# Windowed attention with a rational feed-forward layer: the score matmuls of two half blocks interleaved over the four quarters of the TensorE array

## The chip, the cores and the metric

The kernel runs on one core of a Trainium2 chip. The metric is the device time of one execution in microseconds (us), smaller being better. The kernel before took 675.06 us (median of 3 runs, 675.04 to 675.08). One further execution was taken with the hardware profiler on; every row of a profile in this document comes from such an execution.

## The reference

Inputs are q, k and v of 4 batches, 8 heads, 768 positions and head dimension 64, and the weights of a feed-forward layer. What is computed, in short:

```python
block, window, scale = 32, 16, 1 / sqrt(64)
k_sum = k in blocks of 32, max over the block          # 24 per head
v_sum = v in blocks of 32, mean over the block
scores_l = scale * q @ k.T, masked to |i - j| < 16
scores_s = scale * q @ k_sum.T + log(32)
a = softmax(concat(scores_l, scores_s))
x = (a @ concat(v, v_sum)) as (3072 tokens, 512)
h = x @ w_in                                            # 2048 wide
g = (a0 + a1 h + a2 h^2 + a3 h^3) / (1 + |b0| |h| + |b1| h^2)
out = g @ w_out
```

## The kernel before

**Two halves of work.** The feed-forward layer takes 6 groups of 512 tokens; each group runs over 16 slices of the hidden width, so there are 96 steps (the loop at line 523), and a step's second layer is issued three steps later (`LAG`). Its numbers are split into a high and a low part, so each step has 12 matmuls of 128x128 by 512 for `h` (`moe1`, line 364) and 12 for `po` (`moe2`, line 403). Between them lies the gelu-like function of a step (`gelu`, line 376): on ScalarE (ACT) tiles `tq`, `ta`, `tu` from `h`, on VectorE (DVE) products of `tu` with `h`, and `gh`; on GpSimd (POOL) `gl`. `h` has two buffers in PSUM (`ps_h`), so the matmuls of `h` two steps on wait until DVE has read `h` for the last time, in `tu<-tu,cs,h`.

**The attention** is made in half blocks of 64 queries, 48 of them, numbered `jj`; eight give the tokens of one group. A half block sees 96 keys around its queries and 24 block maxima, 120 columns (`NK`). Its 8 heads lie in 4 head pairs (`NPAIR`): of a pair, head e = 0 lies on SBUF partitions 0 to 63 and head e = 1 on 64 to 127, for q (`qw`) and for the keys (`kw`). `scores` (line 195) is a generator. First it issues 8 matmuls, for each pair `pr` and each `e`, with q as the stationary operand (64x64) and the keys as the moving one (64 rows, 120 columns), in full fp32, into partitions `e * 64` to `e * 64 + 63` of one PSUM tile `sc` (one bank, 480 of 512 columns used). Such an fp32 matmul is two records in the trace, since TensorE makes it in two passes; in the compiled program the two passes of a matmul stand one behind the other. Then DVE adds the mask and takes each row's minimum (4 reads `ss<-sc,mask`, one for each pair), ACT makes the exponentials (4, `ss<-ss,sm`), DVE the reciprocal of the sum, and POOL multiplies by it.

**What follows a half block.** `turned` transposes `ss` on TensorE with an identity (`pt`), ACT copies it out as `pts`, 120 keys on partitions and, for each pair, 64 queries of e = 0 and then 64 of e = 1 along the columns. `both_values` (line 284) multiplies with the values of two half blocks at once: 16 fp32 matmuls `av`, each of 120 rows, 64 columns of the array and 64 moving columns, where e selects the output partitions and the columns of `pts`.

**Order.** Up to step 13 all engines follow an order written out by hand (`EARLY`, `STEP`); half blocks 0 to 15 are done there, and there `scores` issues its own matmuls, before and after the change. From step 14 (`NSTRICT`) only TensorE (PE) keeps the order of the text, and a scheduler orders ACT, DVE and POOL. In this part, every fourth step (14, 18, ..., 74, sixteen of them, `start_of` at line 506) makes the scores of two half blocks, 16 to 47 in pairs. PE's order in such a step is: 12 matmuls of `h`, 16 of `av` for the two half blocks of four steps before (from step 18 on), the 16 of `sc`, 12 of `po`. The transposes of the first of the two half blocks stand two steps later between the `po`, those of the second three steps later. PSUM tiles `sc` and `pt` share a pool of two buffers (`ps_a`).

Lines of a helper that records every operation (`Kept`) stand as L85 in all rows, so instructions are told apart by their tiles: `sc<-kw,qw` are the score matmuls of half blocks 8 to 47.

Of the kernel before, what the change touches and what calls it, by code (L numbers as in the profile page):

```python
# [8 lines left out]
F32 = mybir.dt.float32  # L9
# [9 lines left out]
B, H, S, D = 4, 8, 768, 64  # L19
# [3 lines left out]
P = 128  # L23
NPAIR = H // 2
NCC = DM // P
NFC = DFF // P
HQ = 64
# [3 lines left out]
NK = NKW + NB  # L31
# [26 lines left out]
def tile_kernel(ctx, tc, qw_in, kraw, kwin, vpad, vred, wio, a, b, cmask, cident, cavg, out):  # L58
# [10 lines left out]
    ps_o = ctx.enter_context(tc.tile_pool(name="ps_o", bufs=TPG, space=PSUM))  # L69
    ps_h = ctx.enter_context(tc.tile_pool(name="ps_h", bufs=2, space=PSUM))  # L70
    ps_a = ctx.enter_context(tc.tile_pool(name="ps_a", bufs=2, space=PSUM))
# [23 lines left out]
    pe, dve, act, gps = Kept(nc.tensor), Kept(nc.vector), Kept(nc.scalar), Kept(nc.gpsimd)  # L95
# [7 lines left out]
    kw = [const.tile([P, NKC, NPAIR, NB], F32, name=f"kw{i}") for i in range(2)]  # L103
    qw = [const.tile([P, NPAIR, HQ], F32, name=f"qw{i}") for i in range(2)]
# [80 lines left out]
    def att_load(jj):  # L185
        bi, j = divmod(jj, NJ)
        nc.sync.dma_start(out=qw[jj % 2], in_=qw_in[bi, j])
        nc.sync.dma_start(out=kw[jj % 2][:, 0:NKC - 1], in_=kwin[bi, j])

    def key_blocks(jj):  # L190
        bi, j = divmod(jj, NJ)
        if j < 2 and bi > 0 or jj in (HPG, HPG + 1):
            dve.tensor_copy(kw[jj % 2][:, NKC - 1], ksum[bi])

    def scores(jj, early=False):

        bi, j = divmod(jj, NJ)
        kt, qt = kw[jj % 2], qw[jj % 2] if jj >= HPG else qres[:, jj]
        mt = mask[:, 0 if j == 0 else (2 if j == NJ - 1 else 1), :]
        sc = ps_o.tile([P, 512], F32, tag="o", name=f"sc{jj}") if early else ps_a.tile([P, 512], F32, tag="a", name=f"sc{jj}")  # L200
        for pr in range(NPAIR):
            if jj >= HPG:
                keys = ((0, NK, kt[:, :, pr, :]),)
            else:
                keys = ((0, NKW, kres[:, pr, j * HQ:j * HQ + NKW]), (NKW, NK, ksum[0][:, pr, :]))
            for lo, hi, k in keys:
                for e in range(2):
                    rows = slice(e * D, (e + 1) * D)
                    pe.matmul(sc[rows, pr * NK + lo:pr * NK + hi], qt[rows, pr, :], k[rows], start=True, stop=True)
        yield  # L210
        pool, tag = (gp, "gl") if early and jj % 2 else (pp, "p")
        ss = pool.tile([P, NPAIR, NK], F32, tag=tag, name=f"ss{jj}")
        sm = sp.tile([P, 2, NPAIR], F32, tag="sm", name=f"sm{jj}")
        for pr in range(NPAIR):
            dve.tensor_tensor_reduce(
                out=ss[:, pr, :], in0=sc[:, pr * NK:(pr + 1) * NK], in1=mt, op0=ALU.add, op1=ALU.min,
                scale=-SCALE, scalar=3.0e38, accum_out=sm[:, 0, pr:pr + 1])
        yield
        for pr in range(NPAIR):
            act.activation(ss[:, pr, :], ss[:, pr, :], AF.Exp, scale=-1.0,  # L220
                           bias=sm[:, 0, pr:pr + 1], accum_out=sm[:, 1, pr:pr + 1])
        act.activation(sm[:, 1, :], sm[:, 1, :], AF.Copy, bias=1e-9)
        yield
        dve.reciprocal(sm[:, 1, :], sm[:, 1, :])
        yield
        for pr in range(NPAIR):
            gps.tensor_scalar(ss[:, pr, :], ss[:, pr, :], sm[:, 1, pr:pr + 1], 1.0, op0=ALU.mult, op1=ALU.mult)
        att[jj] = ss
# [55 lines left out]
    def both_values(j0):  # L284

        g, hh = divmod(j0, HPG)
        if hh == 0:
            x32[g] = xp.tile([P, NCC, GT], F32, tag="x", name=f"x{g}")
        av = ps_h.tile([P, NPAIR, 2, HQ], F32, tag="h", name=f"av{j0}")
        for k in range(2):  # L290
            pts = att.pop(j0 + k)
            for pr in range(NPAIR):
                for e in range(2):
                    pe.matmul(
                        av[e * D:(e + 1) * D, pr, k, :],
                        vw[k][:, (2 * pr + e) * D:(2 * pr + e + 1) * D],
                        pts[:, pr, e * HQ:(e + 1) * HQ], start=True, stop=True)
        act.copy(x32[g][:, :, hh * HQ:(hh + 2) * HQ], av.rearrange("p r k q -> p r (k q)"))

    def split(g):  # L300
        if g == 0:
            return x32[0]
        xh = xp.tile([P, NCC, GT], F32R, tag="xh", name=f"xh{g}")
        xl = xp.tile([P, NCC, GT], F32R, tag="xl", name=f"xl{g}")
        for c in range(NCC):
            act.copy(xh[:, c], x32[g][:, c])
            dve.tensor_tensor(xl[:, c], x32[g][:, c], xh[:, c], op=ALU.subtract)
        return xh, xl
# [154 lines left out]
    def lead(chain, all_of=False):  # L463
        for _ in chain or ():
            if not all_of:
                return
# [9 lines left out]
    def whole(jj):  # L476
        yield from scores(jj)
        yield
        yield from values(jj)
# [29 lines left out]
    halves = {}  # L509
# [13 lines left out]
    for step in range(NG * NFC + LAG):  # L523
        g, fc = divmod(step, NFC)
        strictly = step < NSTRICT
        if step == NSTRICT:
            strict -= {dve, act, gps}
            for chain in [c for k, c in sorted(chains.items(), key=str)] + [gelus.pop(s) for s in sorted(gelus)]:
                lead(chain, True)
        if g < NG:  # L530
            if fc == 0:
                with tc.high_priority(offset=60):
                    x = split(g)
            gh, gl, gelus[step] = moe1(g, fc, *x)
            queue.append((g, fc, (gh, gl)))
        for what in STEP.split() if strictly else ():
            kind, n = what[0], int(what[1:] or 0)
            if kind == "g":
                lead(gelus.get(step - n))
            elif kind == "q":  # L540
                lead(prods.get(step - n))
            elif kind == "h":
                for jj in halves.get(step - n, ()):
                    lead(chains.setdefault(("h", jj), whole(jj)))
            elif kind == "k":
                for jj in halves.get(step - n, ()):
                    if jj > HPG + 1:
                        key_blocks(jj)
            elif kind == "l":
                for jj in halves.get(step - n, ()):  # L550
                    load_v(jj)
            elif kind == "a":
                for jj in halves.get(step - n, ()):
                    att_load(jj + 2)
            elif kind == "w" and fc + n < NFC and g == 0:
                lead(chains.setdefault(("w", fc + n), w_split(fc + n)))
            elif kind == "u":
                for f, *args in reduces.get(step, ()):
                    f(*args)
                for f, *args in loads.get(step, ()):  # L560
                    f(*args)
            elif kind == "P":
                pt = (z for jj in halves.get(step - n, ()) for z in turned(jj))
                po = second_layer(step, queue, po, pt)
                lead(pt, True)
            elif kind == "v" and step < LAG:
                if step == 0:
                    vf = ps_o.tile([P, DM], F32, tag="o", name="vf1")
                for i in range(2 * step, 2 * step + 2):
                    value_average(vf, fv1, i)  # L570
                if step == LAG - 1:
                    second_means(vf)
        if strictly:
            continue
        if step in gelus:
            with tc.high_priority(offset=-15):
                lead(gelus.pop(step), True)
        with tc.high_priority(offset=40):
            if step - 4 >= NFC - 2 and halves.get(step - 4):
                both_values(halves[step - 4][0])  # L580
            for jj in halves.get(step, ()):
                key_blocks(jj)
                lead(scores(jj), True)
            for jj in halves.get(step, ()):
                load_v(jj)
                if jj + 2 < NHALF:
                    att_load(jj + 2)
        pt = (z for k in range(2) for jj in halves.get(step - 2 - k, ())[k:k + 1] if jj >= 2 * HPG for z in turned_copied(jj))
        po = second_layer(step, queue, po, pt)
        with tc.high_priority(offset=40):  # L590
            lead(pt, True)
        for f, *args in reduces.get(step, []) + loads.get(step, []):
            f(*args)
# [56 lines left out]
```

## Time and profile before

| | before |
|---|---|
| median of 3 runs | 675.06 us |
| the profiled execution's own time | 674.83 us |
| its span, first to last instruction | 673.0 us |
| mean granted TensorE clock in it | 0.986 |
| PE busy | 655.2 us (97%) |
| DVE busy | 574.9 us (85%) |
| ACT busy | 473.7 us (70%) |
| POOL busy | 263.6 us (39%) |

PE are the matmuls, PEld the loads of stationary operands, which overlap them. A row of the timeline has start, length, engine, operation, tiles as out<-in, shape, count, and in brackets the idle time ahead of it with what ended it; equal instructions in a row are merged, and the length goes to the end of the last. A matmul's record is longer than the distance to the next one, since they are pipelined: distances between starts say what a stream costs. A row of the windows has the window, its length, and for each engine the busy time with the number of instructions. The span's 1.8 us less than the execution's time lies ahead of the first and behind the last instruction.

### The profile page before, as it was taken

Reading aid. Unit: us, or ns where it says so; the run is one execution under the profiler, and the core shown is the slowest. Engines: PE = TensorE matmul, PEld = TensorE weight load, DVE = VectorE, ACT = ScalarE, POOL = GpSimd, SP = SyncE. Lnnn points to the kernel's source line nnn. Section 1 sums busy time; section 2 is a strip of 40 time slices with the busy share of each in tenths; the row PEclk is TensorE's granted clock in tenths of the full one; section 3 lists DMA queues with packets and bytes.
Section 4 is the critical chain, followed back from the end, with each engine's and each line's share of the span. In section 5 each row is a group of like instructions: output and inputs, shape, how many; then the busy total and the mean of one; then the engine's idle time right before and its main releaser. Section 6 shows DMA issues by size and latency. Waiting matters only on the chain.

```text
span 673.0 us, 11873 instructions
## 1 busy us (share of the span) xinstructions
PE 655.2 (97%) x4196; PEld 522.7 (78%) x4196; DVE 574.9 (85%) x1116; ACT 473.7 (70%) x1068; POOL 263.6 (39%) x318
## 2 busy tenths in 40 slices
PE   8897989998999999999999999999999999999997
PEld 5675767776878888888888888888788788888886
DVE  4579999998899989977889988878987778988885
ACT  3869879877867668766667677567686576675563
POOL 1736566835334145244244234333442342222221
PEclk9988989999999999999999999999999999999999
DMA  9997644311224302212114222012031000010001
GB/s 322 331 299 243 221 157 146 140 49 62 94 79 118 127 23 70 67 60 64 56 33 132 87 87 69 21 44 63 0 127 64 0 25 1 1 63 1 0 1 63
DMA packets 29671, 60.75 MB, mean 90 GB/s; under 512 B 3636, under 2 KB 15284, under 8 KB 27692
## 3 DMA queue, kind: packets, MB, share of 16 engines
q1 hardware_dynamic: 28908, 59.54, 27.1%
q8 instruction: 33, 0.54, 0.3%
q10 hardware_dynamic: 576, 0.25, 0.2%
q14 instruction: 26, 0.21, 0.1%
q0 software_dynamic: 128, 0.20, 0.1%
HBM read 53.44 MB, written 6.34 MB: 89 GB/s over the span
## 4 chain that ended last, share of the span: by engine, by line
PE 82%; DVE 8%; DMA 3%; ACT 3%; issue 2%; POOL 1%; SPq 0%; DVEq 0%; ACTq 0%
PE po L85 36%; PE h L85 34%; PE sc L85 6%; PE av L85 3%; PE pt L85 3%; DVE tu L85 2%; DMA wr<-in_wio_dram 2%; DVE tq L85 2%; DMA kres<-in_kraw_dram 1%; DVE wr L85 1%; DVE gh L85 1%; PE vf L85 1%; ACT ta L85 1%; ACT ss L85 1%; DVE w L85 1%
## 5 line engine op out<-in xcount | busy, mean ns | idle before, releaser
L85 POOL TENSOR_TENSOR gl<-tu,ta 128x512 fp32r<-128x512 f32 x96 | 128.3, 1337 | 289.9 <-DVE tu L85 159.9
L85 POOL TENSOR_SCALAR ss<-ss,sm 128x120 f32<-128x120 f32 x192 | 107.1, 579 | 101.5 <-DVE sm L85 101.3
L85 DVE SCALAR_TENSOR_TENSOR tq<-tq,cs,ta 128x512 f32<-128x512 f32 x96 | 106.3, 1107 | 38.9 <-ACT ta L85 38.3
L85 ACT ACTIVATE tq<-h 128x512 f32<-128x512 f32 x96 | 57.2, 596 | 107.1 <-PE h L85 104.3
L85 PE MATMUL po<-wearly,gh 128*128 128x512 f32 x384 | 130.2, 421 | 0.0
L85 PE MATMUL po<-w,gh 128*128 128x512 f32 x384 | 126.7, 411 | 0.0
L85 ACT ACTIVATE ta<-tq,cs 128x512 f32<-128x512 f32 x96 | 69.7, 726 | 50.0 <-DVE tq L85 49.5
L85 PE MATMUL h<-xh,wearly 128*128 128x512 f32 x384 | 96.8, 393 | 1.7 <-DVE tu L85 1.1
L85 PE MATMUL h<-xh,w 128*128 128x512 f32 x384 | 95.1, 390 | 0.0
L85 DVE SCALAR_TENSOR_TENSOR gh<-tu,cs,ta 128x512 fp32r<-128x512 f32 x96 | 77.5, 807 | 18.5 <-ACT ta L85 9.9
L85 PEld LDWEIGHTS h<-xh,wearly 128*128 128x128 f32 x384 | 71.7, 188 | 19.9 <-DVE tu L85 1.6
L85 PEld LDWEIGHTS h<-xh,w 128*128 128x128 f32 x384 | 72.1, 188 | 15.5
L85 ACT ACTIVATE ss<-ss,sm 128x120 f32<-128x120 f32 x192 | 73.3, 386 | 10.8 <-DVE sm L85 10.0
L85 PEld LDWEIGHTS po<-wearly,gh 128*128 128x128 f32 x384 | 66.4, 193 | 17.7 <-issue 2.6
L85 PEld LDWEIGHTS po<-w,gh 128*128 128x128 f32 x384 | 65.9, 189 | 16.9 <-issue 1.3
L85 PE MATMUL po<-w,gl 128*128 128x512 f32 x192 | 75.4, 392 | 1.0 <-POOL gl L85 1.0
L85 PE MATMUL po<-wearly,gl 128*128 128x512 f32 x192 | 76.2, 397 | 0.0
L85 ACT ACTIVATE tu<-h,cs 128x512 f32<-128x512 f32 x96 | 74.9, 781 | 0.0
L85 DVE SCALAR_TENSOR_TENSOR tu<-tu,cs,tq 128x512 f32<-128x512 f32 x96 | 72.0, 750 | 2.7
L85 DVE SCALAR_TENSOR_TENSOR tu<-tu,cs,h 128x512 f32<-128x512 f32 x96 | 71.4, 744 | 2.2
L85 DVE SCALAR_TENSOR_TENSOR tq<-tq,gh 128x512 f32<-128x512 f32 x96 | 66.6, 694 | 3.2
L85 ACT ACTIVATE ta<-h,cs 128x512 f32<-128x512 f32 x96 | 65.5, 682 | 4.2 <-POOL gl L85 4.2
(68 smaller groups left out, 972.1 us busy)
## 6 DMA issues: line engine op xcount, KB each, us to landing
wr<-in_wio_dram SPq DMA_DIRECT2D x15, 1024.0 KB, 6.9
vw<-in_vpad_dram SPq DMA_DIRECT2D x42, 192.0 KB, 2.8
kw<-in_kwin_dram SPq DMA_DIRECT2D x40, 192.0 KB, 3.3
out_dram<-o SPq DMA_DIRECT2D x24, 256.0 KB, 2.1
qw<-in_qw_dram SPq DMA_DIRECT2D x40, 128.0 KB, 3.2
kr<-in_kraw_dram SPq DMA_DIRECT2D x12, 384.0 KB, 3.0
vr<-in_vred_dram SPq DMA_DIRECT2D x8, 384.0 KB, 3.4
vf<-in_vpad_dram SPq DMA_DIRECT2D x2, 1024.0 KB, 12.2
```

Of the source, the lines that this page charges most:

```text
L85: out = getattr(self.engine, name)(*args, **kw)
```

## The change

A new function `both_scores` issues the 16 score matmuls of two half blocks k = 0, 1, in place of the 8 and 8 that `scores` issued one half block behind the other. Both `sc` tiles are taken first. The loop goes over pairs, in a pair over k, then over e. For k = 0 head e goes to output partitions `e * 64` as before. For k = 1 it goes to the other ones: head 0 (rows 0 to 63) to partitions 64 to 127, head 1 (rows 64 to 127) to 0 to 63. Of the array's four quarters of 64 rows by 64 columns, k = 0 takes the two on one diagonal and k = 1 the two on the other. `scores` then goes on with a tile that is ready. The heads of the second half block are swapped on the partitions of `sc`, `ss`, and so along the columns of `pts`; `both_values` reads them back with `e ^ k`. Half blocks 0 to 15 are untouched. No operation is added or removed.

```diff
+    def both_scores(j0):
+
+        tiles = [ps_a.tile([P, 512], F32, tag="a", name=f"sc{j0 + k}") for k in range(2)]
+        for pr in range(NPAIR):
+            for k in range(2):
+                for e in range(2):
+                    rows, q = slice(e * D, (e + 1) * D), e ^ k
+                    pe.matmul(tiles[k][q * HQ:(q + 1) * HQ, pr * NK:(pr + 1) * NK], qw[k][rows, pr, :],
+                              kw[k][rows, :, pr, :], start=True, stop=True)
+        return tiles
+
-    def scores(jj, early=False):
+    def scores(jj, early=False, sc=None):
...
-        sc = ps_o.tile([P, 512], F32, tag="o", name=f"sc{jj}") if early else ps_a.tile([P, 512], F32, tag="a", name=f"sc{jj}")
-        for pr in range(NPAIR):
+        ready = sc is not None
+        if not ready:
+            sc = ps_o.tile([P, 512], F32, tag="o", name=f"sc{jj}") if early else ps_a.tile([P, 512], F32, tag="a", name=f"sc{jj}")
+        for pr in range(0 if ready else NPAIR):
...
-                        pts[:, pr, e * HQ:(e + 1) * HQ], start=True, stop=True)
+                        pts[:, pr, (e ^ k) * HQ:(e ^ k) * HQ + HQ], start=True, stop=True)
...
-                lead(scores(jj), True)
+            for jj, sc in zip(halves.get(step, ()), both_scores(halves[step][0]) if step in halves else ()):
+                lead(scores(jj, sc=sc), True)
```

On PE in step 30 (half blocks 24 and 25; `h1_14` is slice 14 of group 1, `kw0` and `kw1` are the keys of the two half blocks), the rows before are:

```order
L85 MATMUL h1_14_2720<-xl1_1801,w14_1566 128x512 x4
L85 MATMUL av22_2750<-pts22_2669,vw0_100 64x64 x8
L85 MATMUL av22_2750<-pts23_2718,vw1_101 64x64 x8
L85 MATMUL sc24_2769<-kw0_96,qw0_98 64x120 x8
L85 MATMUL sc25_2795<-kw1_97,qw1_99 64x120 x8
L85 MATMUL po1_0_2070<-w10_1260,gh1_11_2593 128x512 x2
L85 MATMUL po1_0_2070<-w10_1260,gl1_11_2594 128x512
```

And now, with two more turns of the same two rows left out:

```order
L85 MATMUL h1_14_2720<-xl1_1801,w14_1566 128x512 x4
L85 MATMUL av22_2750<-pts22_2669,vw0_100 64x64 x8
L85 MATMUL av22_2750<-pts23_2718,vw1_101 64x64 x8
L85 MATMUL sc24_2770<-kw0_96,qw0_98 64x120 x2
L85 MATMUL sc25_2771<-kw1_97,qw1_99 64x120 x2
L85 MATMUL sc24_2770<-kw0_96,qw0_98 64x120 x2
L85 MATMUL sc25_2771<-kw1_97,qw1_99 64x120 x2
...
L85 MATMUL po1_0_2070<-w10_1260,gh1_11_2593 128x512 x2
L85 MATMUL po1_0_2070<-w10_1260,gl1_11_2594 128x512
```

The two `x8` have become four turns of `x2` and `x2`, one turn for each head pair; all else on PE stands as it stood, in all steps.

On DVE in the same step (each `ISA ss` row stands four times, with an `ISA sm` row behind it, of which one pair is shown), the rows before are:

```order
L85 SCALAR_TENSOR_TENSOR tq1_14_2736<-tq1_14_2736,cs_95,ta1_14_2735 128x512
L85 TENSOR_TENSOR tu1_14_2737<-tu1_14_2737,h1_14_2720 128x512
L85 ISA ss24_2778,sm24_2779<-sc24_2769,mask_93 128x120
L85 ISA sm24_2779 128x1
...
L85 SCALAR_TENSOR_TENSOR tu1_14_2737<-tu1_14_2737,cs_95,h1_14_2720 128x512
L85 ISA ss25_2804,sm25_2805<-sc25_2795,mask_93 128x120
L85 ISA sm25_2805 128x1
...
L85 SCALAR_TENSOR_TENSOR gh1_14_2733<-tu1_14_2737,cs_95,ta1_14_2735 128x512
```

And now:

```order
L85 SCALAR_TENSOR_TENSOR tq1_14_2736<-tq1_14_2736,cs_95,ta1_14_2735 128x512
L85 TENSOR_TENSOR tu1_14_2737<-tu1_14_2737,h1_14_2720 128x512
L85 SCALAR_TENSOR_TENSOR tu1_14_2737<-tu1_14_2737,cs_95,h1_14_2720 128x512
L85 ISA ss24_2788,sm24_2789<-sc24_2770,mask_93 128x120
L85 ISA sm24_2789 128x1
...
L85 ISA ss25_2804,sm25_2805<-sc25_2771,mask_93 128x120
L85 ISA sm25_2805 128x1
...
L85 SCALAR_TENSOR_TENSOR gh1_14_2733<-tu1_14_2737,cs_95,ta1_14_2735 128x512
```

The last read of `h` has moved ahead of the first half block's four reads of `sc`. It moves so in ten of the sixteen steps (30, 34, 38, 42 and 54 to 74); in the other six DVE's rows around the scores stand as before. On ACT the four exponentials of a half block now mostly stand together, where before a `ta` often stood behind the first of them. On POOL one `gl` and on SP one load of `kr` change places with a neighbour.

## The prediction

> **What bounds the kernel now.** I read the page's totals first, then its chain of waits:
>
> ```profile
> PE 655.2 (97%) x4196; PEld 522.7 (78%) x4196; DVE 574.9 (85%) x1116; ACT 473.7 (70%) x1068; POOL 263.6 (39%) x318
> ...
> PE 82%; DVE 8%; DMA 3%; ACT 3%; issue 2%; POOL 1%; SPq 0%; DVEq 0%; ACTq 0%
> ```
>
> PE is busy nearly throughout and holds most of the chain. An average says nothing of the sixteen places that change, so I cut the span at the starts of their score blocks (147.08, 176.06, 202.02 and so on, 25.96 us apart). The columns are window, length, then busy us of PE, PEld, DVE, ACT and POOL:
>
> ```profile
> 147.08:176.06 28.98, 26.86 (x169) 20.86 (x168) 26.29 (x53) 21.04 (x48) 12.86 (x13) 1.00 0.16 51
> 176.06:202.02 25.96, 25.96 (x173) 21.08 (x169) 22.85 (x47) 19.61 (x46) 8.71 (x12) 1.00 0.34 112
> 202.02:227.98 25.96, 25.96 (x173) 21.07 (x169) 24.78 (x48) 17.62 (x42) 8.78 (x13) 1.00 0.34 103
> 253.94:279.90 25.96, 25.96 (x173) 21.07 (x169) 23.97 (x46) 19.49 (x46) 12.84 (x15) 1.00 0.15 46
> 357.78:383.74 25.96, 25.96 (x173) 21.08 (x169) 24.70 (x49) 19.37 (x46) 10.53 (x12) 1.00 0.36 102
> 461.62:487.57 25.95, 25.95 (x172) 21.07 (x168) 23.64 (x46) 19.58 (x46) 10.91 (x12) 1.00 0.14 41
> 513.53:539.50 25.97, 25.97 (x173) 21.09 (x169) 19.97 (x42) 17.19 (x42) 8.36 (x13) 1.00 0.13 42
> 539.50:673.04 133.54, 129.70 (x628) 106.53 (x624) 110.92 (x156) 79.28 (x141) 35.08 (x31) 0.99 0.06 20
> ```
>
> From 176.06 on PE fills every window to its last hundredth, at a granted clock of 1.00, and in the rest it lacks 3.84 us of 133.54. These are the fullest windows of DVE, and it still has 1.18 us free in the worst. So a PE block that gets shorter moves all behind it, as long as no cover is used up. Only the first window differs: PE lacks 2.1 us there, and its waits name what is late:
>
> ```profile
> PE h L85 <- DVE tu L85: 1.1, 1, 1.1
> PE po L85 <- POOL gl L85: 1.0, 1, 1.0
> ```
>
> **The block that changes.** One place in the timeline, from the value matmuls through the scores to the next `po`:
>
> ```profile
> 226.89 1.01 PEld L85 LDWEIGHTS av<-pts,vw 120*64 120x64 f32 x32 [0.35 <-issue]
> 226.89 1.15 PE L85 MATMUL av<-pts,vw 120*64 120x64 f32 x32
> ...
> 227.97 1.63 PEld L85 LDWEIGHTS sc<-kw,qw 64*64 64x64 f32 x32
> 227.98 1.86 PE L85 MATMUL sc<-kw,qw 64*64 64x120 f32 x32
> ...
> 229.76 0.73 PE L85 MATMUL po<-wearly,gh 128*128 128x512 f32 x2
> ```
>
> From the first score load to the next `po` it is 229.76 - 227.97 = 1.79 us for 32 passes (16 matmuls of two). What one pass costs alone is in the only large fp32 matmuls, the value means, 512 columns over the whole array; the first row is one run of four passes, the second the records' own length:
>
> ```profile
> 18.41 1.88 PE L85 MATMUL vf<-vf,kres 128*120 128x512 f32 x4
> ...
> L85 PE MATMUL vf<-vf,kres x24: 592/592/690, 14.8 to 56.4; 128*120 128x512 f32 x24
> ```
>
> Starts lie (1.88 - 0.59) / 3 = 0.43 us apart, so a pass of 120 columns takes 0.43 x 120 / 512 = 0.101 us. Thirty-two of them alone would be 3.23 us; the block's 1.79 are 16 x 0.101 = 1.61 plus 0.18 to start and drain. So two passes run at a time already. These are the records of one such block in its first 0.07 us (the window was 227.9 to 228.05, records from 227.97 on):
>
> ```profile
> L85 PEld LDWEIGHTS sc<-kw,qw x4: 129/131/133, 228.0 to 228.0; 64*64 64x64 f32 x4
> L85 PE MATMUL sc<-kw,qw x2: 313/313/313, 228.0 to 228.0; 64*64 64x120 f32 x2
> ```
>
> Two matmul passes have begun where one takes 0.101. Passes of one matmul follow each other (the `vf` rows), so these are those of the two heads, on the two quarters of a diagonal. The other two quarters stand idle in the whole block.
>
> **Part by part.** *The four quarters.* Interleaved, the 32 passes have four targets and need 8 turns of 0.101 where they needed 16. If all four run together a place saves 8 x 0.101 = 0.81 us, and the block is 0.98. The trace has no four at once; the nearest rows bound it. Above: nothing saved, if quarters that share rows or output partitions take turns. Below: 0.81. For rows, `av` is the near case: 32 passes of 120 rows, heads on different output halves, with different moving data, in 1.08 us up to the scores, where 64 columns alone cost 0.054, 1.72 in all. So two streams enter the same rows at once. Two row halves at once are in the score rows themselves, though on different output partitions. Only two row halves that write the same partitions at once, into the two banks of two tiles, have no row. I take 0.81, since each half of the pattern is shown.
>
> *A rule against it.* The records above show a second head's first pass starting ahead of the first head's second pass, though the compiled program has both passes of a matmul one behind the other. The Trainium skill ("TensorE: Matmul & The Clock Gate", Part 3, What overlaps and what doesn't) states that matmuls start and end strictly in program order; by it the new order would run first and second pass as a staircase, two at a time, and save nothing. By that rule this block too would have begun with one pass alone; the trace disagrees, and the sum goes by the trace.
>
> *The loads.* Their number stays at 32 a place. In the `av` rows two loads at a time come every (1.01 - 0.13) / 15 = 0.059 us (0.13 being one load's length, 129 to 133 ns in the rows above). Four a turn, if only two at a time go, take 0.117 where the passes take 0.101: the block is then 8 x 0.117 + 0.18 = 1.12, the saving 0.67. I take four at a time, as the loads go to four quarters.
>
> *How many places.* Fifteen of the sixteen lie where PE has no wait. At the first, in the window from 147.08, `tu` and `gl` are late already, so I count nothing there (0 to 0.81). Sum: 15 x 0.806 = 12.1 us.
>
> *DVE's reads.* All eight reads of a place now find both tiles ready 0.98 us after the block's start; before, the first tile was ready after some 0.9 and the second after 1.79. In ten places the first half block's reads move behind a `tu`. What covers this is the way to the transposes two steps on. The tightest of the fifteen places is also one of the ten:
>
> ```profile
> 257.84 0.73 DVE L85 SCALAR_TENSOR_TENSOR tu<-tu,cs,h 128x512 f32<-128x512 f32 x1
> ...
> L85 POOL TENSOR_SCALAR ss<-ss,sm x4: 793/1049/1339, 261.5 to 264.9; 128x120 f32<-128x120 f32 x4
> ...
> 266.75 0.27 PE L85 MATMUL pt<-ident,ss 128*120 128x128 f32 x1
> ...
> 257.35 0.40 ACT L85 ACTIVATE ss<-ss,sm 128x120 f32<-128x120 f32 x1
> ...
> 257.74 0.61 ACT L85 ACTIVATE ta<-ta 128x512 f32<-128x512 f32 x1
> ...
> 260.54 0.38 ACT L85 ACTIVATE ss<-ss,sm 128x120 f32<-128x120 f32 x1
> ```
>
> POOL's fourth product ends at 264.9 + 0.8 = 265.7, the transposes start at 266.75: 1.06 us of cover, the least of the fifteen. PE comes 0.81 earlier, which leaves 0.25. The moved `tu` puts the first reads up to 0.73 later, but POOL waits for sums that ACT makes behind all eight exponentials, and these, from 257.35 to 260.92, had a 0.61 us `ta` among them that now stands ahead. I take nothing for it; at worst 0.5 us here, once.
>
> *The buffers of `h`.* The least cover between DVE's last read of an `h` and the matmuls two steps on, from 176 on up to step 78, is here:
>
> ```profile
> 369.93 0.75 DVE L85 SCALAR_TENSOR_TENSOR tu<-tu,cs,h 128x512 f32<-128x512 f32 x1
> ...
> 373.84 0.85 PE L85 MATMUL h<-xh,wearly 128*128 128x512 f32 x3
> ```
>
> 373.84 - 370.68 = 3.16 us, four times what a place takes from it, and it does not shrink from place to place while DVE keeps up: the window becomes 25.15 us, and DVE's fullest needs 24.78. ACT and POOL have 6 us and more free in each. `kw` and `qw` were loaded four steps ahead, so SP's queue has no part.
>
> The sum against the profiled execution's 674.83 is 662.7; the median of the runs is 0.23 above that execution, so the forecast is **663.0 us**.
>
> **The rivals.** *Two at a time stays the limit* (no change). Either quarters that share output partitions take turns, or passes start strictly in the program's order, a matmul's first beside the second of the matmul ahead; both ways 16 turns or 17 remain. For it: no row shows two row halves on the same partitions at once. Against it: the parts above, each shown by itself, and for the strict order the two passes in the first 0.07 us. (The second way is what the page's rule would do here.) Both tiles then come ready only at 1.79, the first half block 0.9 later, which with the moved `tu`'s 0.5 uses up the 1.06 at the tightest place and costs some 0.3 us: 675.4. Chance 0.09, of which 0.02 is the strict order.
>
> *Loads take turns in twos.* 15 x 0.67 = 10.1 us: 665.0. For it: the `av` rows never have more than two begun at a time. Against it: there are only two quarters' worth of targets in them. Chance 0.08.
>
> *DVE becomes the bound.* Its gaps are waits for ACT in chains of several steps and may not close: if the four windows with over 23.6 us of DVE give nothing, 11 x 0.81 = 8.9 us remain: 666.2. For it: 24.78 of 25.15 is tight. Against it: the 3.16 us of cover. Chance 0.08.
>
> *A load waits for the other quarter on its rows* (slower). Each row half now always has the other column half's pass running. If a load can't enter rows that are in use, every turn has its 0.059 in the open and no two quarters of a row half overlap: 16 x (0.101 + 0.059) + 0.18 = 2.74 us, 0.95 more than now, 16 times: 15.2 us, 690.3. It decides as soon as turns stay 16 and any part of a load is exposed. Against it: in `av` loads come every 0.059 while passes run on all 120 rows. The Trainium skill (the same page and section) has the rule that a load overlaps a running matmul only where the row groups differ; the `av` rows disagree, so the chance is small: 0.05.
>
> **How the numbers follow.** The forecast has 0.70, the first rival 0.09, the second and third 0.08 each, the last 0.05. The lower end has all sixteen places, 16 x 0.806 = 12.9 us, and half of the 1.1 us that PE waits for `tu` in the first window, should DVE get its scores earlier there: 675.06 - 12.9 - 0.5 = 661.7. The upper end has both partial cases at once, 11 x 0.67 = 7.4 us: 667.7, rounded to 668.0. Forecast and partial cases hold 0.86. What can be told from no change is 0.2%, 1.35 us: faster 0.86, same 0.09, slower 0.05.
>
> **What would show it.** Right: blocks of about 0.98 us from score load to `po`; four matmul passes begun in a block's first 0.07 us or in its second turn; 25.15 us from one place to the next; PE still filling the windows; the first window about as long as before. Wrong: blocks of 1.79 (shared partitions take turns), 1.12 (loads), 2.7 (loads exposed); or short blocks with new PE waits for `ss` at `pt`, or for `tu` at `h`, which would give the time back.

## The result, and the profile after

The changed kernel takes 664.51 us (median of 4 runs, 662.74 to 665.48); the kernel before, in the same comparison, 675.05 us (4 runs, 674.99 to 675.08). The ratio is 0.984, with a 95% interval of 0.9818 to 0.9864: 10.5 us less, where 12.1 were forecast. The profiled execution took 665.48 us (span 663.7), 9.35 less than the one before.

The page's totals and its chain of waits, after:

```profile
PE 643.1 (97%) x4196; PEld 509.9 (77%) x4196; DVE 573.5 (86%) x1116; ACT 475.2 (72%) x1068; POOL 272.6 (41%) x318
...
PE 80%; DVE 8%; DMA 4%; ACT 3%; issue 3%; POOL 1%; SPq 0%; DVEq 0%; ACTq 0%
```

PE lost 12.1 us of busy time with the same 4196 instructions and still holds 80% of the chain: no other engine has become the bound. One place in the timeline of after, the one shown of before:

```profile
227.27 1.01 PEld L85 LDWEIGHTS av<-pts,vw 120*64 120x64 f32 x32 [0.35 <-issue]
227.28 1.15 PE L85 MATMUL av<-pts,vw 120*64 120x64 f32 x32
...
228.35 0.82 PEld L85 LDWEIGHTS sc<-kw,qw 64*64 64x64 f32 x32
228.36 1.05 PE L85 MATMUL sc<-kw,qw 64*64 64x120 f32 x32
...
229.34 0.73 PE L85 MATMUL po<-wearly,gh 128*128 128x512 f32 x2
```

From the score load to the next `po` it is 229.34 - 228.35 = 0.99 us by the rounded rows, 0.98 by their unrounded starts, where it was 1.79. The groups of such a block's first moments (window 228.3 to 228.38, records from 228.35 on):

```profile
L85 PEld LDWEIGHTS sc<-kw,qw x4: 129/130/130, 228.4 to 228.4; 64*64 64x64 f32 x4
L85 PE MATMUL sc<-kw,qw x4: 313/313/314, 228.4 to 228.4; 64*64 64x120 f32 x4
```

Four loads and four passes have begun in 0.03 us, where before only two passes had begun in the first 0.07. The windows from one score block to the next, columns as before (window, length, busy us of PE, PEld, DVE, ACT, POOL, granted clock):

```profile
148.66:177.67 29.01, 26.84 (x169) 20.10 (x168) 26.32 (x53) 21.03 (x48) 12.86 (x13) 1.00 0.16 51
177.67:203.20 25.53, 25.53 (x171) 20.14 (x168) 22.44 (x47) 19.60 (x46) 8.68 (x12) 1.00 0.36 114
203.20:228.36 25.16, 25.16 (x173) 20.29 (x169) 24.13 (x46) 17.62 (x42) 10.89 (x12) 1.00 0.37 106
253.51:278.66 25.15, 25.15 (x172) 20.27 (x168) 23.35 (x46) 19.36 (x46) 12.65 (x14) 1.00 0.16 47
354.12:380.04 25.92, 25.31 (x172) 20.24 (x168) 24.84 (x50) 19.88 (x47) 10.76 (x12) 1.00 0.34 102
530.96:663.68 132.72, 128.88 (x627) 105.75 (x624) 109.68 (x156) 79.45 (x141) 35.35 (x31) 1.00 0.06 20
```

Twelve of the fifteen windows are within 0.01 of 25.15 us, as forecast. Three differ: the first (29.01, before 28.98), step 18's (25.53) and step 46's (25.92). With the starts in these rows and in those of before the 9.35 us can be booked:

| stretch | before | after | difference |
|---|---|---|---|
| ahead of the first place | 147.08 | 148.66 | +1.58 |
| first place to last | 539.50 - 147.08 = 392.42 | 530.96 - 148.66 = 382.30 | -10.12 |
| last place to the end | 133.54 | 132.72 | -0.82 |

The lower two rows make 10.94 us where 12.1 were forecast: 0.38 is missing in step 18's window and 0.77 in step 46's. The first row is a stretch in which the change moves nothing. The waits of PE in after, from 148 to 557, name one that was not there:

```profile
PE h L85 <- DVE tu L85: 1.2, 1, 1.2
PE po L85 <- POOL gl L85: 1.0, 1, 1.0
PE av L85 <- issue: 0.6, 1, 0.6
```

The two upper ones are the first window's, as before. The third is 0.6 us ahead of `av`, the value sums of the half blocks of step 46, at the start of step 50.

### The profile page after: what moved, and what is told of

Read it like the earlier page. It is cut to its first block, busy times and chain, and to the rows that moved or that the text cites. A ratio compares the mean times of both kernels' runs of the same rounds, so it can differ in the third digit from the quotient of the medians.

```text
span 663.7 us, 11872 instructions
## 1 busy us (share of the span) xinstructions
PE 643.1 (97%) x4196; PEld 509.9 (77%) x4196; DVE 573.5 (86%) x1116; ACT 475.2 (72%) x1068; POOL 272.6 (41%) x318
## 4 chain that ended last, share of the span: by engine, by line
PE 80%; DVE 8%; DMA 4%; ACT 3%; issue 3%; POOL 1%; SPq 0%; DVEq 0%; ACTq 0%
PE po L85 36%; PE h L85 34%; PE sc L85 4%; PE av L85 3%; DMA wr<-in_wio_dram 3%; PE pt L85 2%; DVE tu L85 2%; DVE tq L85 2%; DVE wr L85 1%; ACT ta L85 1%; DMA kres<-in_kraw_dram 1%; POOL ss L85 1%; DVE gh L85 1%; DVE ss L85 1%; PE vf L85 1%
## 5 line engine op out<-in xcount | busy, mean ns | idle before, releaser
L85 POOL TENSOR_TENSOR gl<-tu,ta 128x512 fp32r<-128x512 f32 x96 | 134.5, 1401 | 269.5 <-DVE tu L85 175.0
L85 POOL TENSOR_SCALAR ss<-ss,sm 128x120 f32<-128x120 f32 x192 | 110.2, 592 | 105.9 <-DVE sm L85 103.3
L85 DVE SCALAR_TENSOR_TENSOR tq<-tq,cs,ta 128x512 f32<-128x512 f32 x96 | 101.5, 1058 | 28.3 <-ACT ta L85 27.9
L85 DVE SCALAR_TENSOR_TENSOR tq<-tq,gh 128x512 f32<-128x512 f32 x96 | 69.6, 725 | 3.2
## 6 DMA issues: line engine op xcount, KB each, us to landing
vf<-in_vpad_dram SPq DMA_DIRECT2D x2, 1024.0 KB, 12.1
```

Source lines behind the costliest of these rows:

```text
L85: out = getattr(self.engine, name)(*args, **kw)
```

## The experiments

The theory on trial: the gain is the four quarters of the array working at once, 0.81 us at a place. Its rivals: it comes from the two banks or from the order of DVE's and ACT's work, which the interleaving changes as well; quarters that share rows or output partitions do not run together. For what is missing: two covers that the prediction did not see, or scatter. (The cover of a thing is the time by which it is ready before it is needed.)

**The changed kernel again**, unedited, in a second comparison with the kernel before.

> The changed kernel once more, unchanged. Theory A (the spread of its four times, 662.7 to 665.5, comes from where half-clock stretches of TensorE fall in the first 150 us): times again spread over 2 to 3 us, those with the higher mean clock being the shorter, and blocks again 0.98 us; median 663 to 665.5. Theory B (the spread was a disturbance of that chip): times within 0.3 us of each other.

Measured: 664.15 us (663.56 to 664.40, 5 runs) to 675.27 (674.40 to 680.22, 16 runs), ratio 0.982 (0.9794 to 0.9846), 11.1 us less. The profile has blocks of 0.98 us again, and the same two long windows, 25.57 in step 18 and 25.94 in step 46; its first place starts at 147.39, after's at 148.66. So the two windows belong to the kernel, and what lies ahead of step 14 scatters. The five times lie within 0.84 us, less than theory A's 2 to 3 and more than B's 0.3, and the shorter ones do not have the higher clock: neither theory held as written.

Ahead of step 14 the granted clock (third column from the right) falls to half for single stretches; these are the windows from 9 to 30 us of before and of after:

```profile
9.00:30.00 21.00, 19.52 (x326) 14.77 (x328) 13.67 (x80) 16.55 (x69) 12.27 (x27) 1.00 1.06 341
```

```profile
9.00:30.00 21.00, 19.77 (x306) 15.27 (x305) 12.38 (x79) 15.45 (x62) 10.69 (x26) 0.92 1.05 344
```

After has such a stretch here, 3.4 us long at 11.5 us; before has none. By the clock records of the traces all thirteen profiled executions (before, after and the experiments) have three stretches, which start at 31 to 39, 61 to 70 and 88 to 94 us. Only after and one further kernel, the one with the first place left as before, have another at 11 us, of 3.4 and 10.2 us. Only these two reach the first place late, at 148.66 and 152.43 us, where the other eleven reach it at 146.97 to 147.77, 147.28 in the mean: 1.4 and 5.1 us late, about half of each extra stretch. So the 1.58 us go with that stretch in thirteen executions; no experiment set one.

**Interleaved, but not turned**: the loop as in the change, with both half blocks on the old diagonal.

```diff
-                    rows, q = slice(e * D, (e + 1) * D), e ^ k
+                    rows, q = slice(e * D, (e + 1) * D), e
...
-                        pts[:, pr, (e ^ k) * HQ:(e ^ k) * HQ + HQ], start=True, stop=True)
+                        pts[:, pr, e * HQ:(e + 1) * HQ], start=True, stop=True)
```

> Both half blocks' score matmuls interleaved as in the change, but the second's heads not turned: both half blocks use the same two quarters. Theory (the gain is four quarters running at once): 16 turns remain, blocks of 1.79 us, time 674 to 676. Rival (the gain comes from alternating between two PSUM banks or from the other order on DVE and ACT): blocks near 0.98 or the time near 664.

Measured: 675.03 us (673.01 to 676.54, 10 runs), ratio 0.9984 (0.9966 to 1.0002), no change that can be told. One place of its timeline:

```profile
228.14 1.86 PE L85 MATMUL sc<-kw,qw 64*64 64x120 f32 x32
229.93 0.50 PE L85 MATMUL po<-wearly,gh 128*128 128x512 f32 x1
```

1.79 us to the next `po`, as before, and windows of 25.96. This kernel has the change's two banks in turn. By its trace it also has the change's order of ACT's exponentials in all sixteen places, and that of DVE's reads in thirteen (not in steps 18, 22 and 46). It gains nothing: the gain needs the turn.

**Turned, but not interleaved**: all of the first half block, then all of the second on the other diagonal.

```diff
-        for pr in range(NPAIR):
-            for k in range(2):
+        for k in range(2):
+            for pr in range(NPAIR):
                 for e in range(2):
```

> The second half block's heads turned as in the change, but its 8 matmuls issued behind the first's 8. Theory (passes of four quarters must stand near each other in the order): two at a time within each half block and at most one turn saved where they meet, blocks of 1.65 to 1.79 us, time 673 to 676. Rival (PE looks far enough ahead to start the second half block's passes while the first's are queued): blocks near 1.0 and 664.

Measured: 670.39 us (670.29 to 670.58, 5 runs), ratio 0.9916 (0.9887 to 0.9945), windows of 25.61. Hardly anything was expected of it (673 to 676 us), and it brings 0.35 us at a place, a miss. One place:

```profile
228.00 1.51 PE L85 MATMUL sc<-kw,qw 64*64 64x120 f32 x32
229.44 0.73 PE L85 MATMUL po<-wearly,gh 128*128 128x512 f32 x2
```

1.44 us. Two windows within this block, 228.00 to 228.44 and 228.00 to 228.49, show how:

```profile
L85 PE MATMUL sc<-kw,qw x8: 262/263/313, 228.0 to 228.4; 64*64 64x120 f32 x8
```

```profile
L85 PE MATMUL sc<-kw,qw x12: 262/263/313, 228.0 to 228.5; 64*64 64x120 f32 x12
```

Two passes a turn at first, then four within 0.05 us. The starts of the single records lie at 0, 0.153, 0.255, 0.358 and 0.460 us, two each, the second of each two 6 or 7 ns behind the first. At 0.473 and 0.480 two more begin. The first half block's own turns lie 0.10 us apart, so these two are the second's: 10 of the first's 16 passes have begun, 6 are still to come, and the second's go ahead on the free diagonal. So PE starts passes ahead of others that the program has in front of them, while the two diagonals then share turns. With three or four turns shared, 12 or 13 remain of 16: (1.79 - 1.44) / 0.101 = 3.4 turns fewer. On DVE and ACT this kernel's order around the scores is the one of before, and still it gains: what is gained does not come from that order.

**Two orders that keep half of the pattern.** In the first, all matmuls that write partitions 0 to 63 come first, so that the passes of a turn lie on the two row halves and on the same output partitions of two banks; in the second, all of head 0 and then all of head 1, so that the passes of a turn share their rows.

```diff
-        for pr in range(NPAIR):
-            for k in range(2):
-                for e in range(2):
-                    rows, q = slice(e * D, (e + 1) * D), e ^ k
+        for q in range(2):
+            for pr in range(NPAIR):
+                for k in range(2):
+                    e = q ^ k
+                    rows = slice(e * D, (e + 1) * D)
```

```diff
-        for pr in range(NPAIR):
-            for k in range(2):
-                for e in range(2):
+        for e in range(2):
+            for pr in range(NPAIR):
+                for k in range(2):
```

> All 16 matmuls with the change's targets, but ordered so that first only the two quarters that write partitions 0 to 63 have work (head 0 of the first, head 1 of the second half block, into two banks), then only the two that write 64 to 127. Theory (two row halves run at once even on the same output partitions): 16 turns, blocks of 1.79 us, time about 675. Rival (such quarters take turns, and the change gained by another pairing): 32 turns, blocks of 3.4 us, time about 700.

> All 16 matmuls with the change's targets, ordered so that first only the two quarters on rows 0 to 63 have work (head 0 of both half blocks, on different output partitions), then only the two on rows 64 to 127. Theory (any two quarters run at once, and PE looks some matmuls ahead where the two sets meet, as in the order by half blocks): blocks of 1.44 us. Rival (two quarters on the same rows take turns): 2.5 us or more.

Measured: one run each, 673.77 and 670.47 us. The first has a stretch at half clock at 163 us, which makes its first window 32.72, so its time alone says nothing. The blocks do; first the kernel that shares output partitions, then the one that shares rows:

```profile
231.03 1.51 PE L85 MATMUL sc<-kw,qw 64*64 64x120 f32 x32
232.47 0.73 PE L85 MATMUL po<-wearly,gh 128*128 128x512 f32 x2
```

```profile
227.82 1.51 PE L85 MATMUL sc<-kw,qw 64*64 64x120 f32 x32
229.26 0.73 PE L85 MATMUL po<-wearly,gh 128*128 128x512 f32 x2
```

Both 1.44 us, as with the turn alone (1.79 was expected of the first, 1.44 of the second), and in both two passes begin 6 or 7 ns apart in each turn from the start. Passes that share rows run together, and so do passes that write the same partitions of two banks, the half of the pattern for which the prediction had no row. Had either kind taken turns, one pass would have begun where two did.

**The first place left as before** (step 14), all others changed.

```diff
-            for jj, sc in zip(halves.get(step, ()), both_scores(halves[step][0]) if step in halves else ()):
+            for jj, sc in zip(halves.get(step, ()), (both_scores(halves[step][0]) if step > NSTRICT else (None, None)) if step in halves else ()):
```

(`both_values` reads that place's half blocks back unturned.)

> The changed kernel with the first of the sixteen places (step 14) left as before. Theory (there DVE and ACT are late already, and PE only waits longer): its block is 1.79 us again, and yet the first window, from its score load to that of step 18, stays at 28.9 to 29.1 us as with the change. Rival (the place gains its 0.81 as well, and something else in that window was lost with the change): 29.8 us.

Measured: one run, 669.28 us. Its first window, and the one from 9 to 30 us:

```profile
152.43:181.45 29.02, 26.89 (x169) 20.85 (x168) 26.33 (x53) 21.07 (x48) 12.88 (x13) 1.00 0.17 51
```

```profile
9.00:30.00 21.00, 19.75 (x232) 14.27 (x233) 9.58 (x68) 12.50 (x56) 7.51 (x21) 0.76 1.06 345
```

The window is 29.02 us with the old block, 29.01 with the new: the first place gives nothing, as forecast. At its end `av` of step 18 begins 0.10 us behind DVE's last read of `h` in before (174.98 and 174.88) and in after (176.59 and 176.49) alike, so DVE sets where this window ends. The run is 4.8 us over the changed kernel's median, and it is late before the change has any part in it: the first place begins at 152.43, 5.0 behind the 147.39 of the changed kernel's second execution. In the other row PE stood at a granted clock of 0.76, with the stretch of 10.2 us told of above, and got through 232 instructions, where before got through 326. One run of such a kernel can be 5 us off.

**Step 46's window.** In after, the timeline around the new wait, at the end of step 49:

```profile
376.27 1.21 DVE L85 TENSOR_REDUCE vs<-vr 96x32 f32<-96x1024 f32 x1
...
378.11 0.75 DVE L85 SCALAR_TENSOR_TENSOR tu<-tu,cs,h 128x512 f32<-128x512 f32 x1
...
378.96 1.15 PE L85 MATMUL av<-pts,vw 120*64 120x64 f32 x32 [0.61 <-issue]
```

And the same place in before:

```profile
379.34 1.21 DVE L85 TENSOR_REDUCE vs<-vr 96x32 f32<-96x1024 f32 x1
...
381.18 0.75 DVE L85 SCALAR_TENSOR_TENSOR tu<-tu,cs,h 128x512 f32<-128x512 f32 x1
...
382.65 0.56 PE L85 MATMUL av<-pts,vw 120*64 120x64 f32 x11
```

In the code (line 302 of the changed kernel) `av` takes its tile from `ps_h`, the pool of two buffers in which `h` lies. So `av` of step 50 waits for DVE's last read of `h` of step 49, one step back and not two. Before, that read ended at 381.18 + 0.75 = 381.93 and `av` began at 382.65: 0.72 us of cover, by the place's start 24.15 and 24.87. Now PE comes 0.81 earlier, and DVE, which is idle for only 0.9 us from the place's start to this read, before and after, ends its read at 378.86 - 354.12 = 24.74, later by 0.59. That makes 1.40: 0.62 of cover, down to the 0.10 that `av` always begins behind such a read, and 0.78 of wait. Ahead of the read DVE makes the block mean `vs` for the next batch, 1.21 us. Kernels that make the sums of the last batch at earlier steps, four or six ahead, tell whether it is this work.

```diff
-        s = max(start_of(bi * NJ) - SOFF, 0)
+        s = max(start_of(bi * NJ) - SOFF - 4 * (bi == 3), 0)
```

> The changed kernel, with the key and value sums of the last batch made four steps earlier, out of the window of step 46. Theory (the 0.6 us that PE waits at the value matmuls of step 50 is the buffer that they share with h, which DVE's full queue frees late): that wait goes, the window of step 46 falls from 25.92 to 25.15 us, the windows of steps 38 and 42 stay at 25.15; time down by 0.77, to 663.4, which the scatter of the changed kernel half hides, so the window decides. Rival (the wait is for the transposed probabilities or a load): the window stays near 25.9.

Measured with four steps: 665.76 us (663.44 to 667.14, 4 runs), ratio 0.9847 (0.9805 to 0.989). A miss: `av` waits no more, but the window is longer.

```profile
353.01:379.89 26.88, 26.43 (x172) 20.12 (x169) 25.68 (x51) 19.14 (x46) 12.09 (x12) 1.00 0.13 40
...
361.94 1.18 DVE L85 TENSOR_REDUCE vs<-vr 96x32 f32<-96x1024 f32 x1
...
363.04 2.56 DVE L85 TENSOR_TENSOR xl<-x,xh 128x512 fp32r<-128x512 f32 x3
```

A sum still falls into the window, at its step 47, and there it stands ahead of `xl`, the split of the next group's tokens. PE's matmuls of `h` wait for `xl` there, twice, and their loads three times. DVE's work in this window, 25.68 us, is by itself more than 25.15.

With six steps (`- 6 * (bi == 3)`):

> The changed kernel, with the last batch's sums six steps earlier, so that neither the split of step 47 nor the value matmuls of step 50 have one ahead of them on DVE. Theory (DVE frees the buffer that the value matmuls share with h too late, since a sum stands ahead of its last read): window of step 46 25.15 us in place of 25.92, windows of steps 34 to 42 at 25.15 to 25.3; 0.6 to 0.8 us under the changed kernel, 663.5. Rival (that window is bound by the split, with or without sums): it stays over 25.6.

Measured: 664.47 us (664.07 to 667.16, 4 runs), ratio 0.985 (0.9822 to 0.9878). Windows of steps 42, 46 and 50:

```profile
327.60:352.93 25.33, 25.23 (x173) 20.30 (x169) 24.58 (x48) 17.80 (x43) 10.91 (x12) 1.00 0.25 74
352.93:378.07 25.14, 25.14 (x171) 20.26 (x169) 23.54 (x48) 19.31 (x46) 11.78 (x12) 1.00 0.15 43
378.07:403.70 25.63, 25.46 (x172) 20.19 (x168) 20.97 (x45) 19.16 (x46) 8.75 (x13) 1.00 0.25 83
```

Step 46 is down to 25.14, as forecast: the sums on DVE were its whole excess. But step 42 has 0.18 more, since there the next `av` now begins 0.10 us behind DVE's read, and step 50 has 0.48 more: there the first `po` of the next group now waits for ACT's output copies. That PE's stop at `av` had hidden this wait is argued, and fits: step 50 takes 25.61 to 25.63 us in the four kernels without the stop, and 25.14 to 25.17 in the four executions of kernels with it and with blocks of 0.98 us. Of 0.78 us about 0.1 remains from the first place to the last, and the time shows nothing of the 0.6 to 0.8.

**Step 18's window.** The timeline of after at the end of group 0, ACT's copies of the finished outputs and the next group's first `po`:

```profile
184.94 0.57 ACT L85 COPY o<-po 128x512 f32<-128x512 f32 x1
...
185.56 0.30 PEld L85 LDWEIGHTS po<-wearly,gh 128*128 128x128 f32 x2 [0.19 <-ACT o L85]
185.89 0.58 ACT L85 COPY o<-po 128x512 f32<-128x512 f32 x1
186.52 0.30 PEld L85 LDWEIGHTS po<-wearly,gh 128*128 128x128 f32 x2 [0.43 <-ACT o L85]
```

And in before the last two copies, and the loads of the fourth `po`, which are the last row above:

```profile
183.82 1.05 ACT L85 COPY o<-po 128x512 f32<-128x512 f32 x2
...
185.24 0.41 PEld L85 LDWEIGHTS po<-wearly,gh 128*128 128x128 f32 x2
```

Exponentials stand ahead of the last two copies in both. By the place's start the last copy ends at 8.81 us in before (184.87 - 176.06) and at 8.80 in after (186.47 - 177.67): ACT is no later, but PE comes 0.81 earlier. Before, no `po` waited, and the loads of the fourth came at 9.18, a cover of 0.37 us; now they would come at 8.37, and come at 8.85, behind the copy. So this too is a cover that was used up. The edit gives half of group 0's copies to DVE, and a second kernel combines it with the sums four steps earlier:

```diff
-            if g == NG - 1 and t % 2:
+            if g in (0, NG - 1) and t % 2:
                 dve.tensor_copy(o, po[t])
```

> The changed kernel, with two of the four output copies of the first group moved from ACT to DVE. Theory (the window of step 18 is 0.39 us over the others since the next group's first po waits for copies that now stand behind exponentials on ACT): the window falls from 25.53 to 25.15; time down by 0.4. Rival (something on PE itself): it stays at 25.5.

> Both edits together. Theory: all windows from step 18 to 70 at 25.15 us, time 1.1 to 1.2 us under the changed kernel, 663.1 by its median and 662 to 664.5 with its scatter. Rival (the edits move the waits elsewhere): another window grows by as much.

Measured: 664.30 us (661.72 to 665.54, 4 runs), ratio 0.9824 (0.9781 to 0.9867), and with the sums 666.48 (665.30 to 667.63, 6 runs), ratio 0.9865 (0.9827 to 0.9902). Windows of steps 18 and 22 with the copies alone:

```profile
176.33:201.48 25.15, 25.15 (x173) 20.27 (x169) 23.21 (x48) 18.32 (x44) 10.42 (x12) 1.00 0.35 116
201.48:226.94 25.46, 25.22 (x172) 20.30 (x169) 24.27 (x47) 17.84 (x43) 9.28 (x12) 1.00 0.35 105
```

The copies were the whole excess of step 18, and 0.31 of its 0.38 comes back one window on, where `av` now begins 0.10 us behind DVE's read of `h`, as in step 46 of after. The combination is a miss: step 22 takes 25.63, and step 46 is as long as with the four steps alone:

```profile
352.73:379.61 26.88, 26.43 (x171) 20.11 (x168) 25.68 (x51) 19.00 (x45) 12.10 (x12) 1.00 0.13 40
```

The two cures do not help each other. Why step 22, which has none of the moved sums, takes 0.17 more than with the copies alone stays open.

**Six steps earlier, and one copy on DVE**, the fourth of group 0 (`or g == 0 and t == TPG - 1` in place of `g in (0, NG - 1)`).

> That, and the last of the first group's four output copies on DVE in place of ACT. Theory: window of step 18 at 25.15 in place of 25.53 too, with the one of step 22 left at 25.15 since DVE gets one copy less than in the earlier try; 1.0 to 1.2 us under the changed kernel, 663.1 with a scatter of 1 to 1.5. Rival (the window of step 22 gives it back again): 25.3 or more there.

Measured: 664.61 us (663.76 to 665.87, 4 runs), ratio 0.985 (0.9824 to 0.9876). The windows of steps 18 and 22:

```profile
176.08:201.23 25.15, 25.15 (x172) 20.27 (x168) 22.64 (x47) 19.01 (x45) 9.27 (x12) 1.00 0.36 116
201.23:226.44 25.21, 25.21 (x173) 20.31 (x169) 24.14 (x47) 17.68 (x42) 10.88 (x12) 1.00 0.37 106
```

Step 18 is clean and step 22 lost 0.05. From the first place to the last it takes 381.87 us, where after takes 382.30: 0.4 us less. Behind the last matmul this execution and the one with six steps alone have 0.36 us more than after, for a reason that stays open. The times show nothing of the 1.0 to 1.2 us expected. No version here is shown to beat the changed kernel.

## Why the prediction was right, and what it had too large

The sign, the mechanism and the range were right: 664.51 us lies between 661.7 and 668.0, and 1.5 over the forecast of 663.0.

*The block* (16 turns of 0.101 to 8, 1.79 to 0.98 us): right, to the hundredth. *Four loads at a time*: right; the first four begin with their passes, and the rival of loads in twos, 1.12 us, falls. *Two at a time stays the limit* falls by the two orders that share rows or partitions, and a start of passes strictly in the program's order falls by the turn without the interleaving. *A load waits for the other quarter on its rows* falls with the block's 0.98. That the gain is the array's and not the order's is shown by the interleaving without the turn.

*Fifteen of sixteen places count, the first nothing*: right, by the first window's 28.98, 29.01 and 29.02 us.

*DVE's reads of `sc`*, 1.06 us of cover at step 30's transposes: no wait of PE came from it, there or elsewhere. In after POOL's four products of the first half block and the first transpose there:

```profile
261.36 4.18 POOL L85 TENSOR_SCALAR ss<-ss,sm 128x120 f32<-128x120 f32 x4 [5.26 <-DVE sm L85]
...
265.51 0.27 PE L85 MATMUL pt<-ident,ss 128*120 128x128 f32 x1
```

The fourth product ends at 261.36 + 4.18 = 265.54, the first transpose starts at 265.51: the prediction expected 0.25 of the 1.06 us to be left, and nothing is. Still this cost nothing, since the first transpose needs only the first pair's product: the cover reckoned to the fourth was too strict a measure.

*The buffers of `h`* is the step that failed: "The least cover between DVE's last read of an `h` and the matmuls two steps on" was 3.16 us, but `av` is a taker of the same two buffers one step on, with 0.72. It cost 0.77 us, once. DVE's busy time did not tell where: the fullest window, step 22's with 24.78 us, came out at 25.16, and step 46's had 24.70. In after DVE is busy there for 24.84 us of 25.92: PE waited for one read that stood late in DVE's order, as the kernel with the sums six steps earlier shows. The rival of DVE as the bound, priced by four whole windows at 3.2 us, came true for one.

*ACT*: "ACT and POOL have 6 us and more free in each" was true, and still the next group's `po` waited for ACT's copies, which made step 18's window 0.38 us longer. The prediction looked at where DVE's reads move and at the ACT `ta` between exponentials, not at the output copies that ACT makes in the same place, with 0.37 us of cover.

So the term of 12.1 us was mis-sized by 1.16, two covers that it did not list, and measured 10.94 within the profile. Between medians it was 10.5 and, in the second comparison, 11.1. What differs between profiled executions lies mostly ahead of step 14, where an extra stretch at half clock at 11 us goes with a late first place. What sets the time of such a stretch was not tried, and for the runs without a profile no trace shows where their scatter lies.

## What to carry to other kernels

Small matmuls that leave quarters of the array idle gain when a second, independent set takes those quarters in the same turns; reckon the block by turns, and look in its first records for how many passes have begun. Before counting a saving at each place, list every taker of a PSUM pool, by the pool and not by the tile's name, and every copy that frees one, and give each its own cover. A local wait that is taken away comes back at the next cover unless that is looked at too: of 0.78 us in one window 0.1 was kept, of 0.38 in another 0.07.

## What the runs showed of the hardware

PE starts passes out of the program's order where another quarter is free: with 6 passes of one diagonal still to come, two of the other began within 13 ns of the last two of the first, which themselves lay 7 ns apart (1.44 us for a block in place of 1.79). Two fp32 passes of 64x64 by 120 columns run together when they share rows, or when they write the same partitions of two banks; four on the four quarters have turns of 0.10 us, as two on a diagonal had.

The granted clock fell to half for single stretches of 3.4 or 6.8 us three times in the first 100 us of each of thirteen executions (starting at 31 to 39, 61 to 70 and 88 to 94 us), in two of them once more at 11 us (3.4 and 10.2 us), in one at 163 us (6.8 us); the last 2 us of the span are left out here. The two with the stretch at 11 us came to step 14 about half its length late, by 1.4 and 5.1 us.
